# The first weight chunk folded by column halves, and another product at the end of the last group

## The chip, the cores and the metric

The kernel runs on one core of a Trainium2 chip, in one launch. The metric is the device time in microseconds; "before" is the median of four runs.

## The reference

A normalised linear attention feeds a multiplicative feed-forward block.

```python
kv  = einsum('bhsd,bhse->bhde', k, v)            # batch 8, heads 8, seq 576, head_dim 64
out = einsum('bhsd,bhde->bhse', q, kv)
out = out / sqrt(mean(out * out, -1) + 1e-6) * g_norm
x   = out as (4608 tokens, 512)
a, b = x @ w1, x @ w2                            # 512 -> 1024 each
y   = ((a * b) @ w3) @ w_out                     # w3 1024 x 1024, w_out 1024 x 512
```

q, k, v and g_norm are fp32. The four weight matrices come in 64-bit floating point, and the result is fp32.

## The kernel before

Everything is fp32, so TensorE takes each matmul instruction in two passes (the profile counts passes). The order of instructions is written out by hand for TensorE, GpSimd and SyncE throughout, and for VectorE and ScalarE too at the start and, for VectorE, in each group's projection.

**The start: w3 and w_out become one matrix.** Because `(h @ w3) @ w_out = h @ (w3 @ w_out)`, the kernel first computes the 1024 x 512 product of the two, called `w3o_sb`. It runs over `KF` = 8 chunks of 128 columns of w3 (and the same 128 rows of w_out), twice, once for each half of w3's rows. A chunk goes through these steps:

- SyncE loads it (L195): 512 KB of w3 and 512 KB of w_out into one `raw` tile, of which there are four. For chunk 0 each of the two is loaded in two halves.
- Conversion from 64-bit words to fp32: ScalarE makes two parts out of the words (L157 from the low words, L158 from the high words), and VectorE puts them together in four instructions (L160, L164, L167, L170). `begin_next` issues ScalarE's part and `end_next` VectorE's. A chunk is converted in one to three pieces of columns, by the list `cuts`; columns 0 to 511 are w3's and 512 to 1023 are w_out's. L170 is the last step.
- `turn_w3`: TensorE transposes the chunk's w3 blocks (four transposes, L589), and ScalarE copies them out of PSUM (L594).
- `fold_chunk`: four matmuls of 512 columns (L602), one for each 128 rows of the half, accumulate into four PSUM banks over the chunks.

The loop for the first half puts three products of chunk c ahead of the transposes of chunk c + 1, and the fourth behind them. `keep_warm(n)` issues n matmuls of the identity, whose result nobody reads. A transpose turns the row `g_row` into the column `g_col`, which a later scaling of w1 and w2 uses.

**The groups.** The 4608 tokens are worked off in 9 groups of 512. For each, the attention of a later batch is interleaved with the projections by w1 and w2 and with the gate (L623 and the VectorE lines L762, L763), whose result lies in `ab`. Then `project_twice` multiplies `ab` by the folded matrix. Products of matrices are formed by the scheme of Strassen and Winograd, with 7 block products in place of 8; `project_twice` nests it. There are seven outer products, numbered 0 to 6, where 5 is a12 b21 and 6 is a22 t4. Each is made of seven inner products (L900; 28 passes of 128 columns), for which `sum_inner(n)` forms sums on VectorE in four instructions (L858 to L862). `keep` copies a result out of PSUM on ScalarE (L911, L912), `add` adds one to a kept result on VectorE (L939, L940, one for each of two PSUM banks), and `finish(z, half, j)` puts a block of the output together in four VectorE instructions (L921 to L924). The right-hand sides are kept in DRAM as `w3o_l2` and loaded by `load_b`, product for product, on SyncE's queue or ScalarE's.

In the last group one of the seven outer products is not nested: `last_block` computes it plainly, with eight matmuls of 256 columns (L951) behind all others, and adds it to an output block that is otherwise finished. In the kernel before that product is a12 b21. It is formed in two halves of rows, each in its own PSUM bank; after each half VectorE adds (L956) and a store goes out (L933), the first on SyncE's queue and the second on ScalarE's. The block that it completes is `(0, 0)`. Product 6 then takes the place that product 5 has in the other groups:

```python
if last:
    sum_inner(6, place=5)
    finish(p1, 0, 0)
    add(z, r2)
...
products(6 if last else 5, r2)
```

Of the kernel before, what the change touches and what calls it, by code (L numbers as in the profile page):

```python
# [21 lines left out]
def kernel(  # L22
# [44 lines left out]
    N = G // 2  # L67
# [14 lines left out]
    def bank(pool, tag):  # L82
        return pool.tile([P, 512], FP32, name=tag, tag=tag)
# [31 lines left out]
    NF = KF // 2  # L115
# [103 lines left out]
    def conversions(n):  # L219

        what, i = todo[n]
        if what == "w":
            dst = w_sb[:, i].rearrange("p w c f -> p (w c f)")

            return [conversion(n, dst, raws[n], scale=g_col, by_scalar=in_first_group)]
        if what == "b":
            return [conversion(n, chunks[:, 2 * i:2 * i + 2, 0, :], raws[n])]
        dst = chunks[:, i].rearrange("p w f -> p (w f)")
        cuts = [[0, 256, 512, 1024], [0, 512, 1024], [0, 1024]][min(i, 2)]
        return [conversion(n, dst, raws[n], slice(a, b)) for a, b in zip(cuts, cuts[1:])]  # L230

    begun = []
# [350 lines left out]
    w3T = {}  # L583
# [12 lines left out]
    sums_ps = {}  # L596

    def fold_chunk(half, c, ms):
        if c == 0 and 0 in ms:
            sums_ps[half] = [bank(ps_mm, "mm") for m in range(NH)]  # L600
        for m in ms:
            nc.tensor.matmul(  # L602
                sums_ps[half][m], lhsT=w3T[half, c][:, m, :], rhs=chunks[:, c, 1, :],
                start=(c == 0), stop=(c == KF - 1),
            )
            if c == KF - 1:
                nc.scalar.copy(w3o_sb[:, half * NH + m, :], sums_ps[half][m])
# [193 lines left out]
    def prepare_b():  # L801

        nc.sync.dma_start(
            out=w3o_l2[7, :, 0:1024].rearrange("p (f n) -> p f n", n=N), in_=b_blocks()[5]
        )
        for n, y in enumerate(b_blocks()):
            b11, b12, b21, b22 = (
                y[:, 2 * i:2 * i + 2, j * P:(j + 1) * P] for i in range(2) for j in range(2)
            )


            stage = w3o_sums[0].rearrange("p f n -> p (f n)") if n == 4 else (
                o_sbs[(n - n // 5) % 2].rearrange("p m n -> p (m n)")
            )
            stage = stage[:, 0:6 * P]
            t1, t2, t4 = (t.rearrange("p (c n) -> p c n", n=P) for t in (
                stage[:, i * 2 * P:(i + 1) * 2 * P] for i in range(3)
            ))
# [13 lines left out]
    def load_b():  # L832
        n = len(loaded_b)
        if n == ALL_B:
            return
        t = streams[n % len(streams)]

        part = {ALL_B - 2: 6, ALL_B - 1: 7}.get(n, n % 7)

        queue = nc.scalar if n % 7 in (3, 5) else nc.sync  # L840
        if n + 1 < ALL_B:
            queue.dma_start(out=t, in_=w3o_l2[part])
        else:
            t = t[:, 0:1024]
            queue.dma_start(out=t, in_=w3o_l2[part, :, 0:1024])
        loaded_b.append(t)

    inner = {}

    def sum_inner(n, between=lambda: None, place=None):  # L850

        s1, s2, s4 = ab_sums
        x = [ab[0][:, :, 0], s1, s2, s4, ab[0][:, :, 1], ab[1][:, :, 0], ab[1][:, :, 1]][n]
        a11, a12, a21, a22 = (
            x[:, 2 * j:2 * j + 2, i * P:(i + 1) * P] for i in range(2) for j in range(2)
        )
        s1, s2, s4 = inner_sums[(n if place is None else place) % 3]
        nc.vector.tensor_add(s1, a21, a22)  # L858
        nc.vector.tensor_sub(s2, s1, a11)
        nc.vector.tensor_sub(s4, a12, s2)  # L860
        between()
        nc.vector.tensor_sub(a21, a11, a21)  # L862
        inner[n] = [a11, a12, a22, s1, s2, s4, a21]

    def project_twice(T, last, ahead):
# [11 lines left out]

        def products(n, ps=None):

            new = ps is None or n == 5 or last and n == 6  # L880
            if ps is None:
                ps = [bank(ps_mm, "mm").rearrange("p (i n) -> p i n", n=P) for _ in range(2)]
            a11, a12, a22, s1, s2, s4, s3 = inner[n]
            w = loaded_b[7 * done[T] + (5 if last and n == 6 else n)]
            b = w[:, 0:1024].rearrange("p (f n) -> p f n", n=N)
            b11, t3, b21, b22 = (
                b[:, 2 * i:2 * i + 2, j * P:(j + 1) * P] for i in range(2) for j in range(2)
            )
            t1, t2, t4 = (
                w[:, 1024 + 256 * i:1280 + 256 * i].rearrange("p (c n) -> p c n", n=P)  # L890
                for i in range(3)
            )
            seen = set()
            for place, x, y in (
                (0, a11, b11), (3, a12, b21), (1, a22, t4), (2, s1, t1), (6, s2, t2), (5, s4, b22),
                (4, s3, t3),
            ):
# [17 lines left out]
        def finish(z, half, j):  # L915

            def wide(i):
                return z[:, i:i + 1].to_broadcast([P, 2, P])

            dst = o_sbs[half][:, :, j * N:(j + 1) * N].rearrange("p m (i n) -> p m i n", n=P)  # L920
            nc.vector.tensor_add(z[:, 6], z[:, 6], z[:, 0])  # L921
            nc.vector.tensor_add(z[:, 4:6], z[:, 4:6], wide(6))
            nc.vector.tensor_add(dst[:, 1], z[:, 1:3], wide(4))
            nc.vector.tensor_add(dst[:, 0], z[:, 3:6:2], z[:, 0:3:2])  # L924
            if not last:
                if j == 0:
                    store(half)
            elif (half, j) != (0, 0):
                store_block(half, j)

        def store_block(half, j, a=0, b=2, queue=nc.sync):
# [11 lines left out]

        def last_block():

            a12, b21 = ab[1][:, :, 0], loaded_b[7 * done[T] + 6]
            b21 = b21.rearrange("p (f n) -> p f n", n=N)
            for m in range(2):
                ps = bank(ps_at, "at")[:, 0:N]
                for p in range(NF):  # L950
                    nc.tensor.matmul(  # L951
                        ps, lhsT=a12[:, p, m * P:(m + 1) * P], rhs=b21[:, p, :],
                        start=(p == 0), stop=(p == NF - 1),
                    )
                dst = o_sbs[0][:, m, 0:N]
                nc.vector.tensor_add(dst, dst, ps)  # L956
                store_block(0, 0, m, m + 1, nc.scalar if m else nc.sync)


        r1 = products(0)  # L960
# [12 lines left out]
        sum_inner(4)  # L973
        products(3, r2)
        load_b()
        if last:
            sum_inner(6, place=5)

            finish(p1, 0, 0)
            add(z, r2)  # L980
        else:
            add(z, r2)
            sum_inner(5)
        finish(z, 0, 1)
        products(4, r1)
        if last:
# [5 lines left out]
            sum_inner(6)  # L992
            nc.vector.tensor_add(p5, p5, z)
        finish(p5, 1, 1)
        products(6 if last else 5, r2)
        load_b()
        if last:
            add(z, r2)
            finish(z, 1, 0)
            last_block()  # L1000
        else:
            add(p1, r2)
            finish(p1, 0, 0)
            products(6, r1)
            load_b()
            finish(keep("u4", r1), 1, 0)
# [13 lines left out]
    with tc.manual_schedule(  # L1020
# [15 lines left out]
        turn_w3(0, 0)  # L1036
        keep_warm(5)
        begin_next()

        g_ps = bank(ps_at, "at")[:, 0:1]  # L1040
        nc.tensor.transpose(g_ps, g_row, ident[0:1, 0:1])
        nc.scalar.copy(g_col, g_ps)
        for c in range(KF):

            if c == 0:
                end_next()
                begin_next()
            else:
                begin_next()
                end_next()  # L1050
            if c == 4:
                load_kv_left(0)
                load_pair("kvq", 0, 0)
# [3 lines left out]
            fold_chunk(0, c, range(NH - 1))  # L1057
            turn_w3(*((0, c + 1) if c + 1 < KF else (1, 0)))
            fold_chunk(0, c, [NH - 1])
            if c == 0:  # L1060
                keep_warm(4)


        first = batch(0)
# [121 lines left out]
```

## Time and profile before

| | |
|---|---|
| median of four runs | 768.33 us (767.94 to 770.48) |
| the profiled execution's own time | 767.94 us |
| its span in the profile | 766.2 us |
| TensorE's matmuls busy | 758.9 us (99%) |
| VectorE busy | 540.5 us (71%) |
| ScalarE busy | 253.6 us (33%) |
| TensorE's first fold product (chunk 0) | starts at 10.01 us |
| first product of chunk 1, from which TensorE runs on without a gap | starts at 15.58 us |
| last product of the last group | ends near 762.7 us |
| last store issued | 763.19 us |

The profiled execution is the fastest of the four; 1.7 us of its time lie outside the span. Times in the text that name a moment are microseconds from the start of the span. In a line of the timeline the first number is the start, the second the duration, then come the engine, the line of the kernel, the operation, output and inputs with their shapes; in square brackets stands how long the engine was idle before it, and what ended the wait. PE is TensorE's matmul, PEld its weight load, DVE is VectorE, ACT ScalarE, SP SyncE; a q behind a name is that engine's queue of DMA issues. In the chain of work that ended last, a line has the start, the length and what the chain ran through.

### The profile page before, as it was taken

The numbers are of one execution on the slowest core, as the hardware profiler recorded it, in microseconds if no ns is written. First come the engines' busy times: TensorE is split into PE (matmuls) and PEld (weight loads), VectorE is DVE, ScalarE is ACT, GpSimd is POOL, SyncE is SP. The second block draws the span as 40 slices with busy tenths as digits, with TensorE's granted clock in tenths as the row PEclk, the third lists the DMA queues.
The fourth block names the chain that finished last, engine by engine and source line by source line (L and its number), as shares of the span: only waits on it lengthen the run. The fifth ranks groups of instructions, "written<-read, shape, count | busy, mean of one in ns | idle before, by whom it ended". The sixth has DMA issues, their size and how long they took to land.

```text
span 766.2 us, 14426 instructions
## 1 busy us (share of the span) xinstructions
PE 758.9 (99%) x5775; PEld 659.2 (86%) x5775; DVE 540.5 (71%) x1083; ACT 253.6 (33%) x487; POOL 134.7 (18%) x132
## 2 busy tenths in 40 slices
PE   8999999999999999999999999999999999999998
PEld 5455788888899889988998899889988998898897
DVE  7978999438878577756776777567766864495467
ACT  6687753213222332223223321232133222222221
POOL 0000000122610451033114511331144000000000
PEclk9999999999999999999999999999999999999999
DMA  9995641339997844873487548734851470075015
GB/s 317 339 344 172 215 142 39 83 92 261 329 288 259 236 99 123 276 214 97 130 267 202 121 135 268 201 99 130 285 100 43 137 255 1 1 237 156 1 38 190
DMA packets 133159, 132.55 MB, mean 173 GB/s; under 512 B 76644, under 2 KB 121188, under 8 KB 133092
## 3 DMA queue, kind: packets, MB, share of 16 engines
q1 hardware_dynamic: 130640, 116.81, 51.8%
q10 hardware_dynamic: 2452, 14.81, 5.7%
q8 instruction: 46, 0.75, 0.4%
q14 instruction: 21, 0.17, 0.1%
HBM read 100.27 MB, written 16.38 MB: 152 GB/s over the span
## 4 chain that ended last, share of the span: by engine, by line
PE 98%; DMA 1%; ACT 0%; SPq 0%; DVE 0%; issue 0%; ACTq 0%
PE mm L623 60%; PE mm L900 23%; PE mm L602 7%; PE at L332 3%; PE at L415 2%; DMA raw<-in_moe_w_out_dram 1%; PE at L589 1%; PE at L351 1%; PE at L951 0%; DMA raw<-in_moe_w_dram 0%; PE at L448 0%; PE at L433 0%; ACT ab L157 0%; ACT chunks L158 0%; ACT ab L594 0%; SPq L195 0%
## 5 line engine op out<-in xcount | busy, mean ns | idle before, releaser
L623 PE MATMUL mm<-xT,w_sb 128*128 128x256 f32 x768 | 176.2, 379 | 0.0
L623 PEld LDWEIGHTS mm<-xT,w_sb 128*128 128x128 f32 x768 | 145.5, 190 | 20.0 <-issue 0.5
L623 PE MATMUL mm<-xc,ws 128*128 128x256 f32 x576 | 130.2, 379 | 0.0
L623 PEld LDWEIGHTS mm<-xc,ws 128*128 128x128 f32 x576 | 109.4, 190 | 14.9
L762 DVE TENSOR_TENSOR c<-mm,u 128x512 f32<-128x512 f32 x36 | 24.8, 690 | 106.8 <-PE mm L623 106.8
L636 ACT COPY u<-mm 128x512 f32<-128x512 f32 x74 | 43.3, 585 | 138.7 <-PE mm L623 131.3
L636 ACT COPY p<-mm 128x512 f32<-128x512 f32 x74 | 43.3, 585 | 84.7 <-PE mm L623 82.7
L623 PE MATMUL mm<-xc,w_sb 128*128 128x256 f32 x288 | 69.3, 383 | 0.0
L900 PE MATMUL mm<-w3o_sb,raw 128*128 128x128 f32 x500 | 62.3, 275 | 0.0
L602 PE MATMUL mm<-chunks,ab 128*128 128x512 f32 x128 | 60.2, 601 | 1.8 <-DVE chunks L170 1.2
L623 PE MATMUL mm<-xT,ws 128*128 128x256 f32 x256 | 61.1, 381 | 0.0
L290 POOL COPY xT<-xn 128x1024 uint16<-128x1024 uint16 x26 | 32.3, 1270 | 163.3 <-DVE xn L393 163.3
L763 DVE TENSOR_TENSOR ab<-c 128x256 f32<-128x256 f32 x108 | 58.8, 544 | 3.0
L623 PEld LDWEIGHTS mm<-xc,w_sb 128*128 128x128 f32 x288 | 53.6, 190 | 7.8 <-ACT u L636 0.3
L900 PEld LDWEIGHTS mm<-w3o_sb,raw 128*128 128x128 f32 x500 | 59.0, 192 | 0.2 <-DVE raw L858 0.2
L623 PEld LDWEIGHTS mm<-xT,ws 128*128 128x128 f32 x256 | 48.0, 190 | 6.6
L384 DVE TENSOR_REDUCE inv<-sq 128x8 f32<-128x512 f32 (+1 forms) x40 | 23.4, 626 | 37.1 <-ACT sq L383 37.1
L762 DVE TENSOR_TENSOR c<-p,u 128x512 f32<-128x512 f32 x36 | 27.2, 757 | 27.2 <-ACT u L636 27.1
L900 PE MATMUL mm<-w3o_sb,ab 128*128 128x128 f32 x336 | 43.7, 275 | 0.0
L911 ACT COPY u<-mm 128x512 f32<-128x512 f32 x23 | 13.5, 586 | 85.6 <-DVE raw L924 66.4
L602 PEld LDWEIGHTS mm<-chunks,ab 128*128 128x128 f32 x128 | 21.8, 190 | 22.8 <-issue 15.8
L900 PEld LDWEIGHTS mm<-w3o_sb,ab 128*128 128x128 f32 x336 | 41.0, 192 | 0.3
(158 smaller groups left out, 1136.8 us busy)
## 6 DMA issues: line engine op xcount, KB each, us to landing
w3o_sb<-w3o_l SPq DMA_DIRECT2D x26, 896.0 KB, 5.1
raw<-in_moe_w_dram SPq DMA_DIRECT2D x31, 512.0 KB, 7.3
raw<-w3o_l SPq DMA_DIRECT2D x13, 896.0 KB, 4.9
w3o_sb<-w3o_l ACTq DMA_DIRECT2D x11, 896.0 KB, 4.6
k_sb<-in_k_dram SPq DMA_DIRECT2D x32, 256.0 KB, 4.1
v_sb<-in_v_dram SPq DMA_DIRECT2D x32, 256.0 KB, 4.6
q_sb<-in_q_dram SPq DMA_DIRECT2D x32, 256.0 KB, 4.2
out_dram<-raw SPq DMA_DIRECT2D x14, 512.0 KB, 3.6
```

What stands on the lines that cost most here:

```text
L290: nc.gpsimd.tensor_copy(to, src.rearrange("p a n w -> p w a n"))
L332: nc.tensor.matmul(kv_ps[e * D:(e + 1) * D, r - rs[0], :], lhsT=k_sb[:, e, cols] if j < J else kl[:, 2 * r + e, :], rhs=v_sb[:, e, cols] i ...
L351: nc.tensor.transpose(qt_ps[:, e, i, :], q_sb[:, e, i * P:(i + 1) * P], ident)
L384: nc.vector.tensor_reduce(out=inv[:, i], in_=sq.rearrange("p (h d) -> p h d", d=D), axis=AX.X, op=ALU.add)
L415: nc.tensor.matmul(o_ps[l][tokens, n * D:(n + 1) * D], lhsT=qT[r][rows, e, i, tokens], rhs=kv_b[rows, e, r, :], start=True, stop=True,)
L602: nc.tensor.matmul(sums_ps[half][m], lhsT=w3T[half, c][:, m, :], rhs=chunks[:, c, 1, :], start=(c == 0), stop=(c == KF - 1),)
L623: nc.tensor.matmul(ps[:, u, :], lhsT=lhsT(a_name, u, c), rhs=rhs(b_name, c),  start=(u == 0 and c == 0 and to is None), stop=(c == chunks ...
L636: nc.scalar.copy(t, ps)
L762: nc.vector.tensor_add(c, one, two)
L763: nc.vector.tensor_mul(dst, c[:, 0, :], c[:, 1, :])
L900: nc.tensor.matmul(to[:, i, :], lhsT=x[:, c, :], rhs=y[:, c, :], start=new and place // 4 not in seen, stop=(c == 1), skip_group_check=True,)
L911: nc.scalar.copy(t[:, 0:4], ps[0])
```

## The change

It has two parts.

At the start, the w_out half of chunk 0 is converted in two pieces of 256 columns instead of one of 512. The products of chunk 0 are made by halves of w_out's columns: four matmuls of 256 columns for the first half, four for the second, all ahead of chunk 1's transposes (before, three products stood ahead of them and one behind). The copy of chunk 1's transposes now stands ahead of chunk 2's words in ScalarE's order. The transpose of `g_row` moves behind them, and its copy behind chunk 2's words. Six warming matmuls instead of four follow chunk 1's transposes.

At the end, the plain product of the last group is a22 t4 instead of a12 b21, and product 5 is nested as in the other groups. It completes block `(1, 0)`. Both halves of its rows go into one PSUM bank, and the two additions and stores stand behind all of its matmuls. In VectorE's order `add(z, r2)` now stands ahead of `sum_inner(5)`; before, `sum_inner(6)` and `finish(p1, 0, 0)` stood ahead of it. The extra copy in `w3o_l2[7]` is t4 instead of b21.

```diff
-        cuts = [[0, 256, 512, 1024], [0, 512, 1024], [0, 1024]][min(i, 2)]
+        cuts = [[0, 256, 512, 768, 1024], [0, 512, 1024], [0, 1024]][min(i, 2)]
...
-        for m in ms:
+        n = 2 if (half, c) == (0, 0) else 1
+        for h, m in [(h, m) for h in range(n) for m in ms]:
+            cols = slice(h * DM // n, (h + 1) * DM // n)
             nc.tensor.matmul(
-                sums_ps[half][m], lhsT=w3T[half, c][:, m, :], rhs=chunks[:, c, 1, :],
-                start=(c == 0), stop=(c == KF - 1),
+                sums_ps[half][m][:, cols], lhsT=w3T[half, c][:, m, :], rhs=chunks[:, c, 1, cols],
+                start=(c == 0 and h == 0), stop=(c == KF - 1), skip_group_check=True,
             )
...
         def last_block():
-            a12, b21 = ab[1][:, :, 0], loaded_b[7 * done[T] + 6]
+            a22, t4 = ab[1][:, :, 1], loaded_b[7 * done[T] + 6]
...
+            ps = bank(ps_mm, "mm").rearrange("p (m n) -> p m n", m=2)
             for m in range(2):
-                ps = bank(ps_at, "at")[:, 0:N]
                 for p in range(NF):
                     nc.tensor.matmul(
-                        ps, lhsT=a12[:, p, m * P:(m + 1) * P], rhs=b21[:, p, :],
-                        start=(p == 0), stop=(p == NF - 1),
+                        ps[:, m, :], lhsT=a22[:, p, m * P:(m + 1) * P], rhs=t4[:, p, :],
+                        start=(m == 0 and p == 0), stop=(p == NF - 1), skip_group_check=True,
                     )
-                dst = o_sbs[0][:, m, 0:N]
-                nc.vector.tensor_add(dst, dst, ps)
-                store_block(0, 0, m, m + 1, nc.scalar if m else nc.sync)
+            for m in range(2):
+                dst = o_sbs[1][:, m, 0:N]
+                nc.vector.tensor_add(dst, dst, ps[:, m, :])
+                store_block(1, 0, m, m + 1, nc.scalar if m else nc.sync)
...
-        if last:
-            sum_inner(6, place=5)
-            finish(p1, 0, 0)
-            add(z, r2)
-        else:
-            add(z, r2)
-            sum_inner(5)
+        add(z, r2)
+        sum_inner(5)
         finish(z, 0, 1)
...
         finish(p5, 1, 1)
-        products(6 if last else 5, r2)
+        if last:
+            finish(z, 1, 0)
+        products(5, r2)
         load_b()
+        add(p1, r2)
+        finish(p1, 0, 0)
         if last:
-            add(z, r2)
-            finish(z, 1, 0)
             last_block()
...
         for c in range(KF):
             if c == 0:
                 end_next()
+                fold_chunk(0, 0, range(NH))
+                turn_w3(0, 1)
                 begin_next()
-            else:
-                begin_next()
-                end_next()
+                keep_warm(6)
+                g_ps = bank(ps_at, "at")[:, 0:1]
+                nc.tensor.transpose(g_ps, g_row, ident[0:1, 0:1])
+                nc.scalar.copy(g_col, g_ps)
+                continue
+            begin_next()
+            end_next()
...
-            if c == 0:
-                keep_warm(4)
```

More of the change, by code (lines that the diff above doesn't have):

```diff
@@ L803, in prepare_b @@
         nc.sync.dma_start(
-            out=w3o_l2[7, :, 0:1024].rearrange("p (f n) -> p f n", n=N), in_=b_blocks()[5]
+            out=w3o_l2[7, :, 0:1024].rearrange("p (f n) -> p f n", n=N), in_=b_blocks()[6]
         )
@@ L836, in load_b, with sum_inner @@
         t = streams[n % len(streams)]
-        part = {ALL_B - 2: 6, ALL_B - 1: 7}.get(n, n % 7)
         queue = nc.scalar if n % 7 in (3, 5) else nc.sync
         if n + 1 < ALL_B:
-            queue.dma_start(out=t, in_=w3o_l2[part])
+            queue.dma_start(out=t, in_=w3o_l2[n % 7])
         else:
             t = t[:, 0:1024]
-            queue.dma_start(out=t, in_=w3o_l2[part, :, 0:1024])
+            queue.dma_start(out=t, in_=w3o_l2[7, :, 0:1024])
         loaded_b.append(t)
     inner = {}
-    def sum_inner(n, between=lambda: None, place=None):
+    def sum_inner(n, between=lambda: None):
         s1, s2, s4 = ab_sums
@@ L856, in sum_inner @@
         )
-        s1, s2, s4 = inner_sums[(n if place is None else place) % 3]
+        s1, s2, s4 = inner_sums[n % 3]
         nc.vector.tensor_add(s1, a21, a22)
@@ L878, in products @@
         def products(n, ps=None):
-            new = ps is None or n == 5 or last and n == 6
+            new = ps is None or n == 5
             if ps is None:
@@ L883, in products @@
             a11, a12, a22, s1, s2, s4, s3 = inner[n]
-            w = loaded_b[7 * done[T] + (5 if last and n == 6 else n)]
+            w = loaded_b[7 * done[T] + n]
             b = w[:, 0:1024].rearrange("p (f n) -> p f n", n=N)
@@ L927, in finish @@
                     store(half)
-            elif (half, j) != (0, 0):
+            elif (half, j) != (1, 0):
                 store_block(half, j)
@@ L944, in last_block @@
         def last_block():
-            a12, b21 = ab[1][:, :, 0], loaded_b[7 * done[T] + 6]
-            b21 = b21.rearrange("p (f n) -> p f n", n=N)
+            a22, t4 = ab[1][:, :, 1], loaded_b[7 * done[T] + 6]
+            t4 = t4.rearrange("p (f n) -> p f n", n=N)
+            ps = bank(ps_mm, "mm").rearrange("p (m n) -> p m n", m=2)
             for m in range(2):
-                ps = bank(ps_at, "at")[:, 0:N]
                 for p in range(NF):
                     nc.tensor.matmul(
-                        ps, lhsT=a12[:, p, m * P:(m + 1) * P], rhs=b21[:, p, :],
-                        start=(p == 0), stop=(p == NF - 1),
-                    )
-                dst = o_sbs[0][:, m, 0:N]
-                nc.vector.tensor_add(dst, dst, ps)
-                store_block(0, 0, m, m + 1, nc.scalar if m else nc.sync)
+                        ps[:, m, :], lhsT=a22[:, p, m * P:(m + 1) * P], rhs=t4[:, p, :],
+                        start=(m == 0 and p == 0), stop=(p == NF - 1), skip_group_check=True,
+                    )
+            for m in range(2):
+                dst = o_sbs[1][:, m, 0:N]
+                nc.vector.tensor_add(dst, dst, ps[:, m, :])
+                store_block(1, 0, m, m + 1, nc.scalar if m else nc.sync)
         r1 = products(0)
@@ L994, in project_twice @@
         finish(p5, 1, 1)
-        products(6 if last else 5, r2)
+        if last:
+            finish(z, 1, 0)
+        products(5, r2)
         load_b()
+        add(p1, r2)
+        finish(p1, 0, 0)
         if last:
-            add(z, r2)
-            finish(z, 1, 0)
             last_block()
         else:
-            add(p1, r2)
-            finish(p1, 0, 0)
             products(6, r1)
@@ L1038 @@
         begin_next()
-        g_ps = bank(ps_at, "at")[:, 0:1]
-        nc.tensor.transpose(g_ps, g_row, ident[0:1, 0:1])
-        nc.scalar.copy(g_col, g_ps)
         for c in range(KF):
```

## The prediction

> **What bounds the kernel now.** I read the page first, for the span and the chain of work that ended last.
>
> ```profile
> span 766.2 us, 14426 instructions
> PE 758.9 (99%) x5775; PEld 659.2 (86%) x5775; DVE 540.5 (71%) x1083; ACT 253.6 (33%) x487; POOL 134.7 (18%) x132
> PE 98%; DMA 1%; ACT 0%; SPq 0%; DVE 0%; issue 0%; ACTq 0%
> ```
>
> TensorE is busy for 99% of the span and carries 98% of the chain. The change adds and removes no useful matrix work, so it can only move the two ends that TensorE does not carry: the time until its unbroken run begins, and the time from its last product to the last store. Next, the chain in order of time, at the start:
>
> ```profile
> 4.55 8.16 DMA raw<-in_moe_w_out_dram
> ...
> 12.81 1.17 ACT ab L157
> 13.98 1.08 ACT chunks L158
> 15.06 0.48 ACT ab L594
> ...
> 15.58 2.84 PE mm L602 x6
> 18.42 0.44 PE at L589 x4
> ```
>
> The load of chunk 2's w_out lands at 12.71. ScalarE takes chunk 2's words (L157, L158), and only then copies chunk 1's transposed w3 (L594), for which TensorE waits until 15.58. That is the order which the change reverses. The timeline shows what comes directly behind it:
>
> ```profile
> 12.81 1.17 ACT L157 ACTIVATE ab<-raw 128x1024 f32<-128x1024 uint32 x1 [1.59 <-DMA raw<-in_moe_w_out_dram]
> 14.04 1.22 DVE L160 SCALAR_TENSOR_TENSOR ab<-raw,ab 128x1024 uint32<-128x1024 uint32 x1
> 16.62 1.22 DVE L170 CUSTOM_DVE_ANT_0 chunks<-chunks,ab 128x2048 uint16<-128x2048 uint16 x1
> 17.90 0.14 PEld L589 LDWEIGHTS at<-ident,chunks 128*128 128x128 f32 x1 [0.30 <-DVE chunks L170]
> 18.26 0.60 PE L589 MATMUL at<-ident,chunks 128*128 128x128 f32 x4
> ```
>
> Chunk 2's transposes start at 18.26, though TensorE was already waiting for VectorE's last word of that chunk (17.84) at the weight load. Two chains meet there within 0.3 us. At the other end, the timeline of the last group:
>
> ```profile
> 751.81 0.28 DVE L921 TENSOR_TENSOR p<-p 128x128 f32<-128x128 f32 x1
> 753.27 0.68 DVE L939 TENSOR_TENSOR u<-mm,u 128x512 f32<-128x512 f32 x1
> 761.40 0.41 DVE L956 TENSOR_TENSOR raw<-raw,at 128x256 f32<-128x256 f32 x1
> 762.73 0.42 DVE L956 TENSOR_TENSOR raw<-raw,at 128x256 f32<-128x256 f32 x1 [0.92 <-PE at L951]
> 763.19 0.34 ACTq L933 DMA_DIRECT2D out_dram<-raw  x1
> ```
>
> VectorE has no gap over 0.2 us from 740 to 761.8, and is 0.9 us ahead of TensorE's last product (762.70). Whatever takes over 0.9 us of VectorE's cover sets the end.
>
> **The start, step by step.** The first w_out half is issued at 1.77 and lands 4.4 us later, at 6.17; the second lands at 6.9, which piece 3 waited for. In two pieces, VectorE goes on at 6.94, without its 0.62 us idle. A 256-column piece takes 1.34 us (4.28 to 5.62), so chunk 0 is done at 6.94 + 2 x 1.34 = 9.62, against 9.78. VectorE is 0.16 us early in spite of four more instructions.
>
> TensorE: the warming products end about 8.57 as before; the first chunk's eight products of 256 columns are 16 passes at 3.47/16 = 0.217 us (L951's chain row), to 12.04; now they stand wholly ahead of chunk 1's transposes. VectorE has those words at 11.83, so the transposes go at 12.04 instead of 12.66. ScalarE's copy follows a transpose group by 0.64 us (22.21 to 22.85): 12.68. The next L157 follows a copy by 0.50 (0.48 and 0.53 in the rows): chunk 2's words begin at 13.18, where they began at 12.81 when their load had landed. This is the added wait: queued behind it are chunk 2's L157 and L158, and VectorE's whole conversion.
>
> What is won: chunk 1's products start when VectorE has its second half, 9.62 + 2 x 2.13 + 0.08 + 0.06 = 14.02, not 15.58, so 1.56 us earlier. They end at 16.60. What is late next: chunk 2's transposes. From L157 to their weight load is 5.09 us (12.81 to 17.90), and now 13.18 + 5.09 = 18.27, plus 0.11 to the matmul (6.63 to 6.74) = 18.38, against 18.26. After them TensorE's work is the same in both, and VectorE's 3.72 us per chunk is under TensorE's 3.95. So the start costs 0.12 us: the 1.56 us turn into a pause. Bounds: with chunk 2's words at 12.81 as before, the transposes come at 18.01, a gain of 0.25; with chunk 1's transposes as late as before (12.66), a loss of 0.74. I take +0.12, because each step of it has its own row.
>
> At nothing: ScalarE's two more instructions, which lie in a gap that waited for a load (1.62 us before 6.94); the longer warming (four more passes of 0.12 us) in TensorE's pause before 14.02, which is some 1.4 us; g's column, whose 0.15 us copy moves behind chunk 2's words, since the scaling by it comes much later. SyncE issues chunk 4's load when chunk 0's raw words are read, 8.28 + 0.48 = 8.76 instead of 8.41; it lands 9.4 us after its issue, near 18.6, and is used at 19.38. Without that cover it would cost its 0.35 us. The stored extra copy (t4 instead of b21) and the last two loads have the same sizes and places in the queues.
>
> **The end, step by step.** Before, VectorE at 750.08 makes product 6's inner sums (1.73 us) and finishes p1 (1.46), until product 3 is in PSUM. The changed order puts the addition of product 3 first. Its first bank is ready 1.99 us after a product begins and its second 3.33 (product 1 begins at 743.44; the copies L911 and L912 go at 745.43 and 746.77). Product 3 begins at 749.69, so VectorE stands from 750.08 to 751.68, adds, and stands again from 752.28 to 753.02. That is 2.3 us of idle time which the two moved blocks covered. The rest, each by its start-to-start time in the rows: the second addition 0.46 to 753.48; inner sums of product 5, 1.72, to 755.20; finish 1.46, to 756.66; addition of product 4, 1.19, to 757.85; two finishes, to 760.77; addition of product 5, 1.18, to 761.95; finish, to 763.41; the two last additions at 763.41 and 763.75, ending 764.17. ScalarE's issue follows at 764.21 instead of 763.19: 1.02 us late. TensorE is not delayed: product 5's first inner sum is needed near 757.3 and ready by 754.0.
>
> The stores close up too. Before, 384 KB of the last blocks moved from 762.3 to 763.7 and the last 128 KB alone from 764.0 to 764.55 (the DMA row of that window). Now block (0,0)'s 256 KB go out at 763.55 and both 128 KB halves by 764.21; data flowed 0.75 us after an issue, and 524 KB at 350 GB/s take 1.50: done at 765.80 instead of 764.55, 1.25 late. Bounds for the end: 0.34, if only one addition is delayed by its neighbour, and 1.6, if two queues slow each other by as much again as the stores cost over the issue. I take 1.25.
>
> Both halves of the last product now share one PSUM bank, and the order shows the first addition waiting for all 16 passes. In the trace the halves had two banks: the first addition ran at 761.40, with TensorE still in the second half. The Trainium skill, "PSUM — Partial Sum Buffer", section "PSUM bank collisions raise a hardware error", says to guard PSUM by bank and not by address, so one bank must make the addition wait to 762.73; by that rule alone the end would be 0.34 us later. In my sum VectorE only arrives at 763.41, so neither reading alters it.
>
> **The sum.** 0.12 + 1.25 = 1.37 us on the profiled execution's 767.94 (span 766.2 and 1.7 around it): 769.3. That execution is the fastest of four; on their median, 768.33, it is **769.7**.
>
> **Rivals.** (a) *Slower: the clock drops in the new pause.* TensorE stands from 16.60 to 18.38, 1.8 us. The longest pause so far, 1.22 us before 10.01, was followed by products at the full 0.43 us; beyond that the trace shows nothing. The price is a cold start: the first 28 passes took 4.95 us, ten later ones 1.28, so 28 would take 3.58; 1.37 us are lost. Time 769.7 + 1.4 = 771.1. It decides from a pause over 1.22 us. The granted clock is 1.00 in all those rows, so it cannot speak. The Trainium skill, "TensorE: Matmul & The Clock Gate", Part 1, has the clock fall only after an idle window of about 3.4 us; by it this rival costs nothing.
>
> (b) *The start is gained.* If chunk 2's conversion did not hold its transposes, the 1.56 us would stay: 768.33 - 1.56 + 1.25 = 768.0. Against it stands the 17.84.
>
> (c) *VectorE's idle time is absorbed*, and only the shared bank costs: 768.33 + 0.12 + 0.34 = 768.8. For that VectorE would have to reach the last additions by 762.73, 0.7 us sooner than its rows add up to.
>
> **Chances.** Forecast 0.70, (a) 0.13, (b) 0.07, (c) 0.10. A measurement of this kernel tells about 0.3% from no change, 2.3 us: below 766.0 or above 770.6. Forecast, (b) and (c) lie between; (a) and the upper tail of the forecast (start at 0.74 with the end at 1.6 gives 770.7) lie above. Nothing here gives 2.3 us: even (b) with (c) ends at 767.1, so faster gets 0.03, slower 0.20, same 0.77. Range: the forecast's own is 768.9 to 770.7; down to 768.4 for (c) and a run spread of 0.4, up to 771.2 for (a).
>
> **What would show it.** Right: chunk 1's products near 14.0, then a pause, chunk 2's transposes within 0.3 us of 18.3; VectorE idle 2.3 us between 750 and 753; the last addition some 1.0 us later against TensorE's last product, and the last issue too. Wrong: transposes before 18.0 or after 19.0; products slower than 0.43 us after the pause; last addition directly behind TensorE's last product.

## The result and the profile after

The changed kernel took 771.43 us (median of 51 runs, 769.32 to 774.58) and the kernel before 769.00 us (76 runs, 767.24 to 772.96) in the same comparisons. The ratio, that of the means (771.33 and 769.24), is 1.0027, with a 95% interval of 1.0021 to 1.0033: the change costs 2.1 us (1.6 to 2.5), and no part of the interval is a gain. The forecast had 1.4 us, the right sign and less than the interval's lower end. The median itself lies 0.2 us over the forecast's range; the four runs shown beforehand had put the kernel before 0.7 us too low.

The page of the changed kernel, its span, its busy times and the shares of its chain of waits by engine:

```profile
span 772.9 us, 14451 instructions
PE 761.4 (99%) x5787; PEld 662.6 (86%) x5787; DVE 542.6 (70%) x1087; ACT 254.0 (33%) x489; POOL 135.1 (17%) x132
PE 94%; DMA 3%; DVE 2%; issue 0%; ACT 0%; POOL 0%; DVEq 0%; ACTq 0%; POOLq 0%
```

VectorE now has 2% of the chain, where it had nothing, and the DMA engines 3% instead of 1%. The profiled execution took 774.7 us, 3.3 over the median. The list of TensorE's waits tells why it is no typical one (columns: total us, times, longest):

```profile
PE mm L901 <- DMA w3o_sb<-w3o_l: 2.7, 1, 2.7
...
PE at L589 <- DVE chunks L170: 1.3, 1, 1.3
PE mm L901 <- DMA raw<-w3o_l: 0.8, 2, 0.5
```

The 2.7 us are one load of a right-hand side that came in late, near 230 us; the two loads issued there landed 8.5 us after their issue, against a median of 4.5 to 5.1 us for such loads in the page. The clock then fell. This is the product that waited:

```profile
232.93 4.99 PE L901 MATMUL mm<-w3o_sb,raw 128*128 128x128 f32 x28 [2.66 <-DMA w3o_sb<-w3o_l]
```

And these are windows of the same execution (columns: window, its length, then busy time and count of PE, PEld, DVE, ACT and POOL in this order, the granted clock, the DMA share, GB/s):

```profile
232.00:233.76 1.76, 0.83 (x7) 0.86 (x8) 1.55 (x5) 0.00 (x0) 0.00 (x0) 1.00 0.72 267
233.76:237.18 3.42, 3.42 (x18) 3.42 (x17) 1.78 (x4) 0.00 (x0) 0.00 (x0) 0.50 0.89 369
237.18:239.00 1.82, 1.82 (x19) 1.82 (x18) 0.94 (x3) 0.00 (x0) 0.00 (x0) 1.00 0.24 28
```

For 3.4 us TensorE had half the clock, 0.50 in the second row. The 28 passes of that product took 4.8 us from its start to the next one's, where they take 3.1 elsewhere, so the load cost some 1.7 us more than its wait.

The profiles of the experiments have between 0 and 3.4 us of such waits, with the old and with the new order of the ends, and the change leaves that part alone. I count them as noise and read the two ends only. The 1.3 us of L589 are the predicted pause.

The start, in the timeline:

```profile
11.97 0.60 PE L589 MATMUL at<-ident,chunks 128*128 128x128 f32 x4
...
12.61 0.58 ACT L594 COPY ab<-at 128x512 f32<-128x512 f32 x1 [1.34 <-PE at L589]
...
13.09 1.15 ACT L157 ACTIVATE ab<-raw 128x1024 f32<-128x1024 uint32 x1
...
14.02 2.81 PE L605 MATMUL mm<-chunks,ab 128*128 128x512 f32 x6
...
16.86 1.23 DVE L170 CUSTOM_DVE_ANT_0 chunks<-chunks,ab 128x2048 uint16<-128x2048 uint16 x1
...
18.14 0.65 PE L589 MATMUL at<-ident,chunks 128*128 128x128 f32 x4 [1.30 <-DVE chunks L170]
```

Chunk 1's products start at 14.02, as forecast and 1.56 us before the old 15.58. ScalarE's copy stands 1.34 us for TensorE and only then come chunk 2's words, at 13.09 (forecast 13.18, before 12.81). VectorE's last step on that chunk holds the transposes until 18.14 (forecast 18.38, before 18.26). What was won is a pause.

The end, in the timeline of the last group:

```profile
757.17 0.69 DVE L940 TENSOR_TENSOR u<-mm,u 128x512 f32<-128x512 f32 x1 [1.59 <-PE mm L901]
...
758.51 0.56 DVE L941 TENSOR_TENSOR u<-mm,u 128x384 f32<-128x384 f32 x1 [0.65 <-PE mm L901]
...
764.49 3.62 PE L952 MATMUL mm<-w3o_sb,ab 128*128 128x256 f32 x16
...
768.43 0.41 DVE L925 TENSOR_TENSOR raw<-p 128x256 f32<-128x256 f32 x1
768.77 0.74 DVE L958 TENSOR_TENSOR raw<-raw,mm 128x256 f32<-128x256 f32 x2
769.54 0.34 ACTq L934 DMA_DIRECT2D out_dram<-raw  x1
```

The addition of product 3 makes VectorE stand for 1.59 and 0.65 us, 2.24 in all (forecast 2.3). TensorE is through at 768.1, VectorE comes to the two last additions at 768.77 with no gap ahead of them, and the last issue follows at 769.54.

To compare executions whose middles differ, I measure the end from the first pass of the last group's projection. The old end has 22.87 us from there to ScalarE's last issue, in the profile of before and in all eight kernels below that have the old end (22.86 in one). The changed end has 23.81 (its own profile). The last store lands 24.75 to 24.77 us after that first pass in the nine profiles with the old end, and 26.23 us after it in the changed one: 1.5 us later. To the end of the span, which holds the program's exit too, it is 25.6 to 25.8 and 27.2 us.

### The profile page after: what moved, and what is told of

The parts are those of the page before. It is cut to its first block, busy times and chain, and to the rows that moved or that the text cites. A ratio compares the mean times of both kernels' runs of the same rounds, so it can differ in the third digit from the quotient of the medians.

```text
span 772.9 us, 14451 instructions
## 1 busy us (share of the span) xinstructions
PE 761.4 (99%) x5787; PEld 662.6 (86%) x5787; DVE 542.6 (70%) x1087; ACT 254.0 (33%) x489; POOL 135.1 (17%) x132
## 4 chain that ended last, share of the span: by engine, by line
PE 94%; DMA 3%; DVE 2%; issue 0%; ACT 0%; POOL 0%; DVEq 0%; ACTq 0%; POOLq 0%
PE mm L626 60%; PE mm L901 19%; PE mm L605 7%; PE at L332 3%; PE at L415 2%; DMA raw<-w3o_l 2%; DMA w3o_sb<-w3o_l 1%; PE at L589 1%; PE mm L271 1%; PE at L351 1%; PE at L448 0%; PE at L433 0%; DMA out_dram<-raw 0%; DVE chunks L170 0%; DVE ab L160 0%
## 5 line engine op out<-in xcount | busy, mean ns | idle before, releaser
L605 PE MATMUL mm<-chunks,ab 128*128 128x512 f32 (+1 forms) x136 | 60.0, 575 | 0.0
L605 PEld LDWEIGHTS mm<-chunks,ab 128*128 128x128 f32 x136 | 23.5, 190 | 20.2 <-issue 14.8
```

The source lines that it names most:

```text
L605: nc.tensor.matmul(sums_ps[half][m][:, cols], lhsT=w3T[half, c][:, m, :], rhs=chunks[:, c, 1, cols], start=(c == 0 and h == 0), stop=(c == ...
```

## The experiments

**Each part alone.** First the new start with the old end: the first two and the last two hunks of the diff shown above, cut here to their core.

```diff
+        cuts = [[0, 256, 512, 768, 1024], [0, 512, 1024], [0, 1024]][min(i, 2)]
...
+                fold_chunk(0, 0, range(NH))
+                turn_w3(0, 1)
                 begin_next()
+                keep_warm(6)
```

> The kernel before with only the start of the change (chunk 0 by halves of w_out's columns, chunk 1's copy ahead of chunk 2's words). Theory A (the two ends are all of it, and the start swaps one wait for another): within 0.3 us of the kernel before, chunk 2's transposes between 18.0 and 18.5, last store issue 0.48 us after the last product's end as before. Theory B (part of the measured 2 us comes from what the start does to later loads): 0.6 to 1.0 us slower, with TensorE waiting for loads of the folded matrix in the middle.

Measured: 769.35 us, beside 769.24 for the kernel before; ratio 0.9999 (0.9983 to 1.0016). The start brings no gain of 1.56 us (that would be 0.9980, outside the interval). In the profile chunk 3's transposes stand at 22.53, where before had 22.21; its end is the old one, 22.87 us to the issue and 24.75 to the landing.

Then the changed end with the old start, which is the rest of the diff, seen from the kernel before:

```diff
-            a12, b21 = ab[1][:, :, 0], loaded_b[7 * done[T] + 6]
+            a22, t4 = ab[1][:, :, 1], loaded_b[7 * done[T] + 6]
...
-        if last:
-            sum_inner(6, place=5)
-            finish(p1, 0, 0)
-            add(z, r2)
+        add(z, r2)
+        sum_inner(5)
```

> The changed kernel with the start of the kernel before, so only the end of the change. Theory A: 1.3 us slower than before, all of it behind the last group's first nested product (25.7 us from there to the end of the span before, 27.0 after). Theory B: less than the changed kernel's 2 us by 0.6 to 1.0, or, if the extra stored copy of t4 disturbs the middle, the full 2 us.

Measured: 771.12 us; ratio 1.0018 (1.0001 to 1.0034), some 1.4 us. The tail took 23.82 us to the last issue and 26.22 to the landing; chunk 3's transposes stood at 22.29. Nearly all of what this kernel loses is at its end.

**The order on VectorE.** The changed kernel, with the sums again ahead of the addition in the last group:

```diff
-        add(z, r2)
-        sum_inner(5)
+        if last:
+            sum_inner(5)
+            add(z, r2)
+        else:
+            add(z, r2)
+            sum_inner(5)
```

> The changed kernel, but in the last group sum_inner(5) stands ahead of add(z, r2), so that VectorE makes these sums while product 3 is being formed. If VectorE's idle 2.3 us there are the cause of the end's price: VectorE reaches the last additions by the end of TensorE's last product, both follow directly behind it, and the last issue is 0.8 us after that product instead of 1.4; 0.7 to 0.9 us faster than the changed kernel. If the shared bank alone is the cause: no change, since the bank is still shared.

Measured: 770.18 us; ratio 1.0009 (0.9989 to 1.0028). The interval is too wide to rank it by time; the timeline ranks it:

```profile
754.16 0.68 DVE L940 TENSOR_TENSOR u<-mm,u 128x512 f32<-128x512 f32 x1
755.43 0.56 DVE L941 TENSOR_TENSOR u<-mm,u 128x384 f32<-128x384 f32 x1 [0.59 <-PE mm L901]
...
761.42 3.62 PE L952 MATMUL mm<-w3o_sb,ab 128*128 128x256 f32 x16
...
765.07 0.75 DVE L958 TENSOR_TENSOR raw<-raw,mm 128x256 f32<-128x256 f32 x2 [0.35 <-PE mm L952]
765.86 0.34 ACTq L934 DMA_DIRECT2D out_dram<-raw  x1
```

The wait of 1.59 us is gone. VectorE now reaches the last additions first and stands 0.35 us for TensorE: with one PSUM bank the first addition waits for all 16 passes, where with two banks it had run at 761.40 beside the second half. The last issue is 23.20 us from the start of the projection, 0.61 less than in the changed kernel and 0.33 more than before. The last store lands at 25.16, 1.07 less than in the changed kernel and 0.4 more than before.

**Two banks as well.** The same, with last_block's halves in two banks and an addition and a store behind each half:

```diff
-            ps = bank(ps_mm, "mm").rearrange("p (m n) -> p m n", m=2)
             for m in range(2):
+                ps = bank(ps_at, "at")[:, 0:N]
...
-            for m in range(2):
                 dst = o_sbs[1][:, m, 0:N]
-                nc.vector.tensor_add(dst, dst, ps[:, m, :])
+                nc.vector.tensor_add(dst, dst, ps)
```

> As the one before, and the two halves of the last product in a bank each, with addition and store behind each half. If idle VectorE and the shared bank together are the end's price: the last issue 0.5 us after the last product as in the kernel before, and 1.2 to 1.3 us faster than the changed kernel, level with the kernel before within 0.3 us. If the choice of the product itself (a22 t4 in place of a12 b21) costs anything: slower than before by that.

Measured: 770.45 us; ratio 1.0007 (0.9990 to 1.0024). That is not level with the kernel before within the 0.3 us expected, though the interval allows it. The last issue is back at 22.87 us, so the order on VectorE (0.61) and then the shared bank (0.33) make up the whole 0.94 us of the issue. The order of these two steps matters: in the changed kernel VectorE reaches the last additions after TensorE's last pass, so there the bank alone would cost nothing.

The landing does not follow the issue. The last store lands at 25.18, as with one bank (25.16) and 0.4 later than with the old end, although the issue is as early. Here the 256 KB of the block before the last and both halves of 128 KB go out together: the DMA row of the profile shows 334 to 342 GB/s in one unbroken stretch of about 1.5 us, where before had two stretches with a pause between them. With one bank and with two the 256 KB are issued at the same place, 22.10 us from the start of the projection (23.15 in the changed kernel), and the rest queues behind them. So 0.4 us is the price of stores that close up, alone, and the shared bank costs the landing nothing. The start of this execution was late: chunk 3's transposes at 23.31.

**The changed kernel again**, without an edit, to see whether its first profile was typical.

> The changed kernel itself once more, beside the kernel before on this chip. Theory A (start 0, end 1.3 to 1.4 us, the rest is that executions differ in how long TensorE waits for loads of the folded matrix): 1.2 to 1.6 us slower than before. Theory B (start and end together cost more than each alone): 2.0 us or more.

Measured: 771.24 us; ratio 1.0026 (1.0013 to 1.0038). The end repeats, 23.81 us to the issue and 26.27 to the landing. The start does not: chunk 3's transposes at 23.25, where the first profile has 22.15. The delay begins at once, in the warming products. Windows of two us of this execution (columns: window, its length, TensorE busy and its passes, granted clock, DMA share, GB/s):

```profile
2.00:4.00 2.00, 2.00 (x9) 1.00 0.95 277
4.00:6.00 2.00, 2.00 (x12) 1.00 0.92 312
6.00:8.00 2.00, 2.00 (x11) 1.00 1.06 371
8.00:10.00 2.00, 2.00 (x18) 1.00 1.06 385
```

The same windows of before (with the other engines' columns between):

```profile
2.00:4.00 2.00, 2.00 (x9) 2.00 (x10) 0.00 (x0) 0.41 (x3) 0.47 (x1) 1.00 0.90 270
4.00:6.00 2.00, 2.00 (x15) 2.00 (x14) 1.65 (x6) 1.32 (x4) 0.00 (x0) 1.00 0.93 291
6.00:8.00 2.00, 2.00 (x19) 1.80 (x18) 1.31 (x5) 1.06 (x2) 0.00 (x0) 1.00 0.99 344
```

Before, TensorE makes 9, 15 and then 19 passes in these windows. Here it makes 9, 12 and 11, and 18 only from 8 on. The 28 warming passes took 6.28 us instead of 4.95, and chunk 0's transposes came at 8.07 instead of 6.74.

The granted clock is 1.00 in every row, but in the first rows that means only that the trace holds no clock record for the stretch yet. Its first record, of the full clock, begins at 5.26 us in the profile of before and at 8.04 in this one. The passes change with it: start to start they lie 0.213 us apart ahead of the record and 0.112 us behind it, in both. I call the time from TensorE's first pass to this record the cold phase: 3.3 us before, 6.1 us here. This was a new suspect; the next three kernels look at the rest of the start.

**The copy behind chunk 2's words**, in the start alone: `begin_next()` ahead of `turn_w3(0, 1)`.

```diff
-                turn_w3(0, 1)
                 begin_next()
+                turn_w3(0, 1)
```

> The start of the change alone, but ScalarE copies chunk 1's transposes behind chunk 2's words, as in the kernel before; the halves stay. If chunk 2's conversion holds the start: chunk 1's products begin near 15.5 instead of 14.0, chunk 2's transposes stay between 18.0 and 18.3, time as before within 0.3 us. If the copy's place were worth its 1.5 us (the rival that the start is gained): 1.5 us slower than the start alone.

Measured: 769.77 us; ratio 1.0013 (1.0001 to 1.0026). Chunk 1's products started at 16.24 instead of 14.02 and ran straight into chunk 2's transposes, at 18.92 (expected near 15.5, and 18.0 to 18.3); chunk 3's stood at 22.87. A load of w_out landed late in this execution (5.5 us after its issue), so its start is late for two reasons. What it does show is that one wait takes the other's place: TensorE has no pause ahead of chunk 2's transposes and stands 1.30 us ahead of chunk 1's products instead, behind ScalarE's copies.

**A finer cut of chunk 2**, in the start alone, so that its transposes need only the first half of the words:

```diff
-        cuts = [[0, 256, 512, 768, 1024], [0, 512, 1024], [0, 1024]][min(i, 2)]
+        cuts = [[0, 256, 512, 768, 1024], [0, 512, 1024], [0, 512, 1024], [0, 1024]][min(i, 3)]
```

> The start of the change alone, and chunk 2 is converted in two pieces of 512 columns, w3 first, so that its transposes need half of the conversion. If VectorE's conversion of chunk 2 is what TensorE waits for: chunk 2's transposes directly behind chunk 1's third product, near 16.7 instead of 18.1, and then VectorE's chain holds chunk 3's transposes near 22.0; of the 1.4 us at most 0.3 are kept, since two pieces cost VectorE 0.54 us more than one. If something else holds them (the copy, a PSUM bank): 18 as before.

Measured: 769.55 us; ratio 1.0006 (0.9995 to 1.0018). The timeline of TensorE:

```profile
14.51 2.84 PE L605 MATMUL mm<-chunks,ab 128*128 128x512 f32 x6
17.19 0.60 PE L589 MATMUL at<-ident,chunks 128*128 128x128 f32 x4
...
18.82 2.81 PE L605 MATMUL mm<-chunks,ab 128*128 128x512 f32 x6 [0.17 <-DVE chunks L170]
22.54 0.63 PE L589 MATMUL at<-ident,chunks 128*128 128x128 f32 x4 [0.91 <-DVE chunks L170]
```

Now the transposes follow chunk 1's products without a pause, and the pause moves one chunk on. VectorE's conversion is what sets the pace there, and this cut does not keep TensorE's early start. That no other cut would is not shown.

**Without the six warming matmuls** behind chunk 1's transposes, in the start alone:

```diff
-                keep_warm(6)
```

> The start of the change alone, without the six warming matmuls behind chunk 1's transposes: TensorE then stands from about 12.5 to 14.0 and again from 16.7 to 18.1. If pauses of this length let the clock fall (the rival of the forecast): passes of 512 columns of more than 0.43 us after them and 1 us or more slower. If not: 0.43 us throughout and the time as with the start alone.

Measured: 769.50 us; ratio 1.0004 (0.9992 to 1.0017). TensorE stood 1.15 us ahead of chunk 1's products (from 14.17) and 1.54 us ahead of chunk 2's transposes, and the products behind both ran at 0.43 us per pass. The warming is worth nothing that shows, and pauses of 1.15 and 1.54 us did not slow the products behind them.

**A late TensorE, on purpose.** Three kernels, beside the same runs of the kernel before. The first two lengthen the warming, in the old order and in the start alone:

```diff
-        keep_warm(14)
+        keep_warm(22)
```

> The kernel before, with 22 warming matmuls in place of 14 ahead of the first transposes: 16 passes more, at 0.128 us each, hold TensorE 2.05 us longer. This does on purpose, and more strongly, what a long cold phase does. Theory (in the old order a late TensorE is absorbed, since chunk 1's copy stands behind chunk 2's words on ScalarE and these do not wait for TensorE): chunk 0's transposes near 8.8, its products near 10.7 instead of 10.01, chunk 1's transposes near 13.35, but the copy still at about 15.06 and chunk 3's transposes still at 22.2 to 22.3; time within 0.2 us of the kernel before, ratio 1.000. Rival (a late TensorE costs its delay in either order): chunk 3's transposes near 24.2, ratio 1.0027.

Measured: 769.82 us; ratio 1.0008 (0.9998 to 1.0019). This execution fell on a long cold phase (6.2 us), so chunk 0's transposes came 3.15 us late, at 9.89 (before 6.74), and not the 2.05 expected: 16 warm passes at 0.112 us make 1.8 us, and the longer cold phase the rest. Chunk 3's came at 23.85, 1.64 us late and not at the 22.2 to 22.3 expected: the old order absorbed 1.5 us. By the rows the rest came through chunk 1's words, ahead of which TensorE's first copy stands (at 10.53, and the words at 11.01).

> The start of the change alone, the end as before, with the same 22 warming matmuls. Theory (in the new order ScalarE meets chunk 1's copy, and so TensorE's whole chain, ahead of chunk 2's words): everything behind the warming comes 2.05 us later, copy near 14.7, chunk 2's words near 15.1, its transposes near 20.2, chunk 3's near 24.2 (22.15 where the warming was short); time 2.0 us over the start alone without this, so 1.9 to 2.3 us over the kernel before, ratio 1.0025 to 1.003. Rival (the new order has slack as well, and the late profiles had another cause): chunk 3's transposes below 23, ratio below 1.001.

Measured: 770.39 us; ratio 1.0027 (1.0017 to 1.0037). Chunk 0's transposes came at 8.39 and chunk 3's at 23.57: against the changed kernel's first profile, which has 6.65 and 22.15, 1.42 of 1.74 us came through. The delay is less than the 2.05 us expected: 16 warm passes at 0.112 us make 1.8 us, and the cold phase was as short here (3.0 us) as in that profile. Copy and words come later by the same step: 14.04 and 14.52, against 12.61 and 13.09. In time, beside the kernel before, the longer warming costs 0.6 us in the old order and 2.1 us in the new one, and the two intervals hardly touch.

The third shortens it, in the start alone:

```diff
-        keep_warm(14)
+        keep_warm(10)
```

> The start of the change alone, the end as before, with 10 warming matmuls in place of 14 ahead of the first transposes: 8 passes fewer, at 0.17 to 0.23 us each while cold. Theory (what costs is a warming that outlasts VectorE's first two pieces, near 6.57): it ends by 6.3 even in a slow execution, the transposes stand at 6.6 to 6.75, bound by VectorE, chunk 3's at 22.1 to 22.3; time 0.2 to 0.5 us under the start alone, ratio to the kernel before 0.9995 to 1.0000. Rival (what heats TensorE is the number of passes that it made): the passes that are missing are made up for cold further on, chunk 0's 16 products among them, and chunk 3's transposes stay at 22.5 or later.

Measured: 768.97 us; ratio 1.0000 (0.9991 to 1.0008), level with the start alone. The 20 passes took 4.64 us, and the four transposes behind them 1.35 us, part of it a wait for VectorE's second piece. Chunk 3's transposes stood at 22.58. The rival's number came out, but a long cold phase (5.9 us) and a late w_out load (6.83) fell into the same execution; this one decides nothing.

**The warming earlier**, start alone, on a block of ones that VectorE sets:

```diff
+    ones = kv_sb[0][:, 0].rearrange("p a b -> p (a b)")[:, 0:P]
+    nc.vector.memset(ones, 1.0)
...
-        keep_warm(14)
+        keep_warm(14, ones)
```

> The start of the change alone, the end as before, with the first 14 warming matmuls made of a block of ones that VectorE sets, in place of the identity that GpSimd builds: they can begin near 1.1 us instead of 1.95, the same in number. Theory (the cold phase begins with TensorE's first pass, lasts 3.0 to 6.0 us, and costs the new order what it reaches over VectorE's second piece at 6.57): the warming ends between 5.9 and 7.4 instead of 6.8 and 8.3, chunk 0's transposes at 6.6 to 7.4, chunk 3's at 22.1 to 22.6; time 0 to 0.5 us under the start alone, ratio to the kernel before 0.9990 to 1.0000. Rival (the end of the cold phase does not depend on when TensorE begins): the warming takes 0.85 us longer than 4.8 to 6.3 us and chunk 3's transposes spread from 22.15 to 23.3 as they did.

Measured: 769.59 us; ratio 1.0004 (0.9993 to 1.0016). TensorE's timeline:

```profile
1.09 5.91 PE L273 MATMUL mm<-kv_sb 128*128 128x128 f32 x28 [1.09 <-DVE kv_sb L263]
6.84 0.62 PE L591 MATMUL at<-ident,chunks 128*128 128x128 f32 x4
...
18.14 0.66 PE L591 MATMUL at<-ident,chunks 128*128 128x128 f32 x4 [1.31 <-DVE chunks L170]
...
22.16 0.60 PE L591 MATMUL at<-ident,chunks 128*128 128x128 f32 x4
```

The warming was slow again, 5.91 us (a cold phase of 5.3 us), but it began 0.86 us earlier, and chunk 3's transposes stand at 22.16 as in the best executions. In this one profile the mechanism holds. In time nothing can be seen of it (start alone 0.9999, this 1.0004, both within 0.0016), so it is no version to recommend.

None of the versions beats the kernel before.

## Why the prediction was right, and where it was off

**The sign and the mechanism of the end were right, with one term too small.** VectorE's idle time was 2.24 us for 2.3, and the last issue came 0.94 us late (23.81 against 22.87) for the 1.02 of the sum. The term that was mis-sized is the stores' closing up. The sum gave it 0.23 us. From the issue to the landing the last store takes 2.4 us in the three profiles with the changed end and 1.9 in the nine with the old one: 0.5 us. I had counted bytes at one bandwidth from a fixed delay after the issue; the kernel with two banks shows 0.4 us of it with an issue that is not late at all. The end thus costs 1.5 us, not 1.25, still inside its bounds of 0.34 to 1.6. By the landing it splits into 1.07 us for the order on VectorE, which brings the block before the last to its issue 1.05 us late, and 0.4 for the stores that close up.

The lower bound, 0.34 for the shared bank, was the delay of the last issue (0.33 measured) and not of the landing, where the bank costs nothing. So the case of rival (c), VectorE in time and only the bank left, is the kernel with the sums first, and what it pays is the 0.4 us of the stores.

**The start was right in its rows and too small in its mean.** In the changed kernel's first profile every step is within 0.24 us of the forecast, and the loss of 0.12 came out as 0.06 the other way (22.15 against 22.21 at chunk 3's transposes). What the sum lacked is that the old start was not only a sequence but also a buffer. "The warming products end about 8.57 as before" took one execution's cold phase for a constant. In six profiles of the new start with its first warming unchanged (one of them without the six later matmuls) the full clock begins at 5.07, 5.35, 5.84, 6.51, 8.04 and 8.11 us, and chunk 3's transposes stood, in the same order, at 22.15, 22.18, 22.51, 22.53, 23.25 and 23.31, on average 22.66. The two profiles of the old start have 22.21 and 22.29. So the change costs the start 0.4 us on average, as far as six profiles and two can tell. The lengthened warming shows the cause: put ahead of chunk 2's words, ScalarE's copy ties VectorE's whole conversion to TensorE's chain, and 1.42 of 1.74 us come through, where the old order swallowed 1.5 us. The two delays were not of one size (3.15 and 1.74 us). No profile of the old start with its normal warming fell on a long cold phase, so that it would have swallowed one is inferred from the lengthened one.

**The new sum** is 0.4 + 1.5 = 1.9 us, against 2.1 measured (1.6 to 2.5). One thing speaks for less: from the last landing to the end of the span, the program's exit, it is 1.1 us in the three profiles with the old start and 0.9 to 1.0 in the eleven with the new one, so up to 0.2 us come off; why is open. Each part alone was timed too (−0.1 and 1.4 us), but with intervals of 1.3 us either way; the split rests on the profiles.

**The rivals.** (a), the clock that drops in the new pause, fell: the pause came, 1.30 us by the profile (1.8 in the forecast), the products behind it ran at 0.43 us, and the clock record of that execution is full from 5.07 to 233.76 us. Its time, 771.1, was near the result for another reason, and the price it named (1.4 us of cold passes) exists, but at the other side, before the work begins. Its mechanism exists too, for a longer pause: the clock fell to half behind the 2.66 us without work near 230 us in the changed kernel's first profile, and not behind a wait of 2.3 us in the kernel with the finer cut.

The Trainium skill, "TensorE: Matmul & The Clock Gate", Part 1, had spoken against (a) with its idle window of about 3.4 us. The 1.54 us pause without warming agrees as far as it reaches, but the 2.66 us are less than the page's window, and the clock fell all the same, 0.8 us after TensorE had work again. Where the two differ the measurement counts. The same part says that the number of cold matmuls varies from run to run; that row was the one to use, and I used it for the pause alone. Its budget of 3.4 us, with half a microsecond either way, is too tight for these runs, whose cold phases lasted 3.0 to 6.2 us.

(b), the gained start, fell twice: by the time of the start alone, and by the finer cut, where the pause only moves on. (c), VectorE's idle time absorbed, fell too: VectorE comes to the last additions 0.7 us after TensorE's last product, with no gap.

**The shared bank.** The forecast left open whether one bank makes the first addition wait, since VectorE came later anyway. With the sums first VectorE comes earlier, and the addition waits for the last pass (0.35 us idle). That is what the rule of the Trainium skill, "PSUM — Partial Sum Buffer", section "PSUM bank collisions raise a hardware error", gives for a guard by bank.

## What to carry to other kernels

A copy that moves ahead of a load's words ties two chains that had been independent; before such a move, ask how much each chain varies from one execution to the next, and not only when it is done in the one profile. In a tail, let the engine that finishes last do its free work while it would wait. Count stores to their landing, with their neighbours, and not to the last issue alone: here an issue that was 0.33 us earlier landed no earlier, because the block ahead of it was still moving.

## What was not expected of the hardware

TensorE's cold phase took 3.0 to 6.2 us over the fourteen profiles, most of which have the same first instructions. A view that prints a granted clock of 1.00 there has no record behind it; the passes, 0.213 us apart instead of 0.112, tell. From its first record the clock stayed full for 761.17 or 764.58 us in thirteen of the fourteen profiles, two lengths that lie 3.41 us apart, and the half clock in the fourteenth lasted 3.41 us.

Loads of 896 KB, whose median in the page is 4.5 to 5.1 us, took 8.5 us in one execution and cost TensorE a wait of 2.7 us and then some 1.7 us at half the clock. Such waits differ by up to 3.4 us between profiles and hide changes of this size.
